# Two decode layers on one core: the last w2 chunk in 15 transfers, q in 12 slices, x added by five products

## The chip, the core and the metric

The kernel runs on one core of a Trainium2 chip. The time is that of the device, in microseconds, for one launch; three launches of the kernel before took 528.68, 529.14 and 530.48 us, so the median is 529.14. A core has TensorE (PE, matrix products), VectorE (DVE), ScalarE (ACT), GpSimd (POOL) and SyncE (SP, which here issues the loads), and 16 transfer engines that carry out what is issued. The inputs lie in HBM, the working memory (SBUF) and the accumulators of products (PSUM) have 128 partitions.

## The reference

Two layers, each an attention step and a feed-forward step on one token of width 640, with the same weights and the same cache in both layers. `setup_inputs` makes bf16 arrays; the key and value caches have 32 heads of 32768 rows by 192, of which the last 4096 are used.

```python
def _A_ref(x, k_cache, v_cache, wq, wo):
    B, Sq, D = x.shape                       # 1, 1, 640
    Hq, Dh = 32, 192
    Hkv, Sk = k_cache.shape[1], k_cache.shape[2]   # 32, 32768
    W = min(4096, max(256, Sk // 4))         # 4096
    q = (x @ wq).reshape(B, Sq, Hq, Dh).transpose(0, 2, 1, 3)
    k = k_cache[:, :, Sk - W:, :]
    v = v_cache[:, :, Sk - W:, :]
    scores = jnp.einsum("bhqd,bhkd->bhqk", q, k) * (Dh ** -0.5)
    p = softmax(scores, axis=-1)
    o = jnp.einsum("bhqk,bhkd->bhqd", p, v)
    return o.transpose(0, 2, 1, 3).reshape(B, Sq, Hq * Dh) @ wo

def _B_ref(x, w1, w3, w2):                   # 640x1536, 640x1536, 1536x640
    return (silu(x @ w1) * (x @ w3)) @ w2

x = A_x
x = x + _A_ref(layernorm(x), k_cache, v_cache, wq, wo)
x = x + _B_ref(layernorm(x), w1, w3, w2)
x = x + _A_ref(layernorm(x), k_cache, v_cache, wq, wo)
x = x + _B_ref(layernorm(x), w1, w3, w2)
```

## The kernel before

**Pages and loads.** Everything large goes through `arena`, an SBUF tile of 16 slots of 128 x 6144 bf16 (1.5 MB). One slot holds one page: a fifth of `wq`, the 4096 keys or values of one head, up to nine of the 48 chunks (128 x 640) of `wo`, or a piece of `w1`, `w3` and `w2`. The list `loads` has all pages of both layers in the order of use (lines 158 to 191). `refill` (193) takes the next page whenever a slot is free and issues its transfers on SP's queue at line 203; `done(key)` (218) frees a slot after the last product on its page and calls `refill`. Fourteen heads' keys stay in their slots for layer 1 (`RETAIN`), and one more is kept in PSUM (`stash`).

**The order of SP's queue.** `pin` keeps the order of the program on each engine, so SP issues in the order of `loads`. The tile framework gives the transfers eight completion semaphores in turn. An issue therefore waits for three things: its slot, a semaphore (until the load eight places before it has landed), and whatever wrote that slot before.

**The stages of a layer.** `layernorm` gives `xs`; `qproj` (247) multiplies it with the five `wq` pages: per page 16 products of 384 columns in `q_ps`, four abreast in the four column groups of TensorE (`tile_position`), then a copy (260), 12 small products that turn q (264 to 267) and a copy to `qt_sb` (268), from which `build_w` (270) puts the weights of the scores in `wst`. Per head, the keys are turned on VectorE (293) and multiplied; every four heads a softmax follows; the values follow six heads behind. `wo_proj` (392) multiplies the 48 chunks of `wo`. The head blocks are taken in the order `ORDER`, (3, 2, 1, 0) in layer 0 and (1, 0, 2, 3) in layer 1. The last three chunks (45 to 47) are not loaded in layer 1: they are multiplied with `wo5`, which layer 0 loaded for its own chunks 45 to 47, those of block 0.

**Openings.** `y_open` (383) opens the two accumulators of `wo_proj` and of layer 0's `w2` by eight products with `zero`, since later products write one row of each column group.

**The end.** In layer 1 `ffn` (412) prepares `ident`, a 128 x 128 f32 unit matrix in a free slot, on GpSimd; multiplies `w1` and `w3`; computes `htd`, the gated vector, and calls `last_rows` (466). That opens `f_ps` with four zero products, adds x by 20 small f32 products with `ident`, and multiplies `htd` with the twelve `w2` chunks in the order 0 to 3, 9 to 11 (in `keep` since layer 0), 4 to 8. Chunks 4 and 5, 6 and 7, and 8 are layer 1's last three loads (188). A copy (482) and one store of 4 rows of 160 (484) end the program.

Of the kernel before, what the change touches and what calls it, by code (L numbers as in the profile page):

```python
# [7 lines left out]
BF16 = mybir.dt.bfloat16  # L8
F32 = mybir.dt.float32
U32 = mybir.dt.uint32  # L10
ALU = mybir.AluOpType
# [4 lines left out]
P = 128  # L16
D = 640
NCH = 5
H = 32
# [4 lines left out]
HB = 4  # L24
NB = H // HB
PGW = 6144
# [15 lines left out]
def _ap(t, p0, npart, off, dims):  # L42
    ps = t.ap[0][0]
    return bass.AP(t.tensor, t.offset + p0 * ps + off, [[ps, npart]] + [list(d) for d in dims])
# [3 lines left out]
def kernel(  # L48
# [13 lines left out]
    nc = tc.nc  # L62
# [9 lines left out]
    m_ps = pss[:, MB:MB + MN]  # L72


    def pin(ins):
        tc.keep_in_program_order(ins)
        return ins

    def mm(*a, **k):
        return pin(nc.tensor.matmul(*a, **k))  # L80
# [17 lines left out]
    nc.gpsimd.memset(sel4[:], 0.0)  # L98
    nc.gpsimd.affine_select(out=sel4[:], in_=sel4[:], compare_op=ALU.not_equal, fill=1.0, base=0,
                            pattern=[[-32, 4]], channel_multiplier=1)  # L100
    sel16 = cst.tile([P, 4, 4], BF16, name="sel16")
    nc.gpsimd.memset(sel16[:], 0.0)
    nc.gpsimd.affine_select(out=sel16[:], in_=sel16[:], compare_op=ALU.not_equal, fill=1.0, base=0,
                            pattern=[[-32, 4], [-1, 4]], channel_multiplier=1)


    sel = cst.tile([P, 2, HB, 16], BF16, name="sel")
# [23 lines left out]
    zero = cst.tile([P, 32], BF16, name="zero")  # L131
    nc.gpsimd.memset(zero[:], 0.0)
    w20 = cst.tile([P, 768], BF16, name="w20")
    qt_sb = cst.tile([P, 2, 6, 16], BF16, name="qt_sb")
    rl = cst.tile([P, 1], F32, name="rl")


# [7 lines left out]
    loads = []  # L145
# [9 lines left out]
    def head(layer, g):  # L155
        return HG * ORDER[layer][g // HG] + g % HG

    for layer in range(2):
        for c in range(NCH):
            loads.append((("q", layer, c), [(0, PGW, wq_v[c])]))  # L160
        for i in range(H + LEAD):
            for kind, g, cache in (("v", i - LEAD, A_v_cache), ("k", i, A_k_cache)):
                if not 0 <= g < H:
                    continue
                h = head(layer, g)
                if kind == "k" and layer == 1 and h in RETAIN:
                    if h == STASH:
                        loads.append((("k", 1, h), []))
                    continue
                loads.append(((kind, layer, h),  # L170
                              [(0, PGW, cache[0, h, S0:SK, :].rearrange("(p t) d -> p (t d)", p=P))]))
        for w in range(6):
            parts, ci, end = [], 9 * w, min(9 * w + 9, 48)
            while ci < end:
                to = min(end, ci - ci % 12 + 12)
                parts.append((640 * (ci - 9 * w), 640 * (to - ci),
                              wo_v[ORDER[layer][ci // 12]][:, 640 * (ci % 12):640 * (ci % 12 + to - ci)]))
                ci = to
            if w < 5:
                loads.append((("o", layer, w), parts))  # L180
            elif layer == 0:
                assert len(parts) == 1 and parts[0][1] == 1920
                loads.append((None, [(wo5[:], parts[0][2])]))
        loads.append((("fa", layer), [(0, PGW, w1_v[:, 0:PGW])]))
        loads.append((("fb", layer), [(0, PGW, w3_v[:, 0:PGW])]))
        loads.append((("fc", layer), [(0, 1536, w1_v[:, PGW:]), (1536, 1536, w3_v[:, PGW:]),
                                      (3072, 2560, w2_v[:, 0:2560])]))
        fd = [(0, 3200)] if layer == 0 else [(0, 1280), (1280, 1280), (2560, 640)]
        loads.append((("fd", layer), [(o, n, w2_v[:, 2560 + o:2560 + o + n]) for o, n in fd]))
        if layer == 0:  # L190
            loads.append((None, [(keep[:], w2_v[:, 5760:7680])]))

    def refill():
        while loads and (free or loads[0][0] is None):
            key, parts = loads.pop(0)
            if key is None:
                for dst, src in parts:
                    pin(nc.sync.dma_start(out=dst, in_=src))
                continue
            s = free.pop(0)  # L200
            home[key] = s
            for off, n, src in parts:
                pin(nc.sync.dma_start(out=arena[:, s * PGW + off:s * PGW + off + n], in_=src))  # L203
            if not parts:
                stash(arena[:, s * PGW:s * PGW + PGW], False)

# [40 lines left out]
    def qproj(layer):  # L247
        q_ps = ps_a.tile([P, 512], F32, tag="a", name="q_ps")
        for c in range(NCH):
            pg = page(("q", layer, c))  # L250
            for c2 in range(4):
                for j in range(4):
                    hp = 4 * j + c2
                    mm(q_ps[32 * j:32 * j + 32, 0:384], lhsT=xs[:, c, 3 - c2:35 - c2],
                       rhs=pg[:, 384 * hp:384 * hp + 384],
                       start=(c == 0 and c2 == 0), stop=(c == NCH - 1 and c2 == 3),
                       tile_position=(0, 32 * j))
            done(("q", layer, c))
        q_sb = w20
        pin(nc.scalar.copy(out=q_sb[:, 0:384], in_=q_ps[:, 0:384]))  # L260
        qt_ps = m_ps[0:32].rearrange("p (h i c) -> p h i c", h=2, i=6)
        for hh in range(2):
            for it in range(6):
                be, par = divmod(it, 2)
                o = 64 * (3 * hh + be) + par
                mm(qt_ps[:, hh, it, :], lhsT=q_sb[:, o:o + 63:2],
                   rhs=sel16[:].rearrange("p j c -> p (j c)"), start=True, stop=True)
        pin(nc.vector.tensor_copy(out=qt_sb[0:32], in_=qt_ps[:]))  # L268

    def build_w(b, first):  # L270
        engs = (nc.gpsimd, nc.scalar) + ((nc.vector, nc.vector) if first else (nc.gpsimd, nc.scalar))
        for a in range(4):
            dst = _ap(wst[:], 32 * a, 32, 8 * a + HB - 1, [[382, HB // 2], [191, 2], [32, 6]])
            src = _ap(qt_sb[:], 0 if first else 32 * a, 32, HB // 2 * b, [[1, HB // 2], [96, 2], [16, 6]])
            pin((engs[a].copy if engs[a] is nc.scalar else engs[a].tensor_copy)(out=dst, in_=src))  # L275
        if first:
            for a in range(1, 4):
                pin(nc.vector.tensor_copy(out=qt_sb[32 * a:32 * a + 32], in_=qt_sb[0:32]))
# [104 lines left out]
    def y_open(name):  # L383

        y_ps = [ps_a.tile([P, 512], F32, tag="a", name=f"{name}{i}") for i in range(2)]
        for nh in range(2):
            for j in range(4):
                mm(y_ps[nh][32 * j:32 * j + 32, 0:320], lhsT=zero[:], rhs=ptm[:, 0:320],
                   start=True, stop=False, tile_position=(0, 32 * j))
        return y_ps  # L390

    def wo_proj(layer):
        y_ps = y_open("y_ps")
        for w in range(6):
            pg = page(("o", layer, w)) if w < 5 else wo5
            for cc in range(min(9, 48 - 9 * w)):
                ci = 9 * w + cc
                j = ci % 4
                for nh in range(2):
                    mm(y_ps[nh][32 * j:32 * j + 1, 0:320], lhsT=otd[:, ci:ci + 1],  # L400
                       rhs=pg[:, 640 * cc + 320 * nh:640 * cc + 320 * nh + 320],
                       start=False, stop=(ci >= 44), tile_position=(0, 32 * j))
            if w < 5:
                done(("o", layer, w))
        y_to_residual(y_ps)
# [6 lines left out]
    def ffn(layer):  # L412
        if layer == 1:
            assert not loads
            spare = free[0] * PGW
            ident = arena[:, spare:spare + 256].bitcast(F32)
            nc.gpsimd.memset(ident, 0.0)
            nc.gpsimd.affine_select(out=ident, in_=ident, compare_op=ALU.not_equal, fill=1.0, base=0,
                                    pattern=[[-1, P]], channel_multiplier=1)
        g_ps = ps_a.tile([P, 512], F32, tag="a", name="g_ps")  # L420
        u_ps = ps_a.tile([P, 512], F32, tag="a", name="u_ps")
        for ps, kind, c0, c1, off in ((g_ps, "fa", 0, 4, 0), (u_ps, "fb", 0, 4, 0),
# [42 lines left out]

    def last_rows(ident):
        f_ps = ps_a.tile([P, 512], F32, tag="a", name="f_ps")
        for j in range(4):
            mm(f_ps[32 * j:32 * j + 32, 0:160], lhsT=zero[:], rhs=ptm[:, 0:160], start=True, stop=False,
               tile_position=(0, 32 * j))  # L470
        for c in range(NCH):
            for j in range(4):
                mm(f_ps[32 * j:32 * j + 1, c:160:NCH], lhsT=xsq[:, c:c + 1], rhs=ident[:, 32 * j:32 * j + 32],
                   start=False, stop=False, tile_position=(0, 32 * j))
        for fcx in (0, 1, 2, 3, 9, 10, 11, 4, 5, 6, 7, 8):
            pg, off = w2_chunk(1, fcx)
            for j in range(4):
# [77 lines left out]
```

## Time and profile before

| what | value |
|---|---|
| three launches, us | 528.68, 529.14, 530.48 |
| profiled launch: span, us | 527.83 |
| mean granted clock of TensorE | 0.72 |
| busy: PE, DVE, ACT, POOL, us | 275.8, 256.5, 62.3, 14.3 |
| bytes read, MB | 221.6 |
| GB/s, mean over the span | 421 |
| GB/s, typical slice in the middle | 430 |
| last landing of `w2`, us | 524.36 |
| store issued, us | 525.08 |
| store landed, us | 526.74 |

The span is that of one profiled launch, from the program's first instruction to its last; the launches that were timed take 1.31 us more in the median. All times inside the launch count from the span's start. The landing times are those of the semaphores' updates; a load of 128 rows makes 16, one of each transfer engine, and has landed with the last. A line such as `L80 PE MATMUL` names line 80 of the kernel, the helper `mm` through which all products go, so products are told apart by the tiles they write. Of SP, the duration is that of issuing, not of the transfer.

### The profile page before, as it was taken

The page shows a single profiled execution, that of the slowest core. Times are in us where ns is not written, and L with a number is a line of the kernel's source. Part 1 is how long each engine was busy: PE and PEld are TensorE (multiplying, and loading weights), DVE is VectorE, ACT ScalarE, POOL GpSimd, SP SyncE. Part 2 cuts the span into 40 slices and gives each one's busy share as a digit, 9 for nine tenths or more (in the row PEclk, how much of TensorE's full clock was granted, in tenths as well). Part 3 has the DMA queues.
Part 4 walks back from the last instruction along what each step waited for, and adds up shares of the span by engine and source line. Part 5 has one row for each costly group of instructions (what it writes and reads, how often), then busy time and mean ns, then how long its engine had stood idle before and what let it go on. Part 6 is the DMA issues. An engine that isn't in the chain of part 4 may idle for free.

```text
span 527.8 us, 6132 instructions
## 1 busy us (share of the span) xinstructions
PE 275.8 (52%) x2487; PEld 113.9 (22%) x2487; DVE 256.5 (49%) x393; ACT 62.3 (12%) x192; POOL 14.3 (3%) x66
## 2 busy tenths in 40 slices
PE   2354644463645555455445446678254655446545
PEld 1111212121212221122112212233121322112212
DVE  1199676656656475754001139431475654753001
ACT  1002020111102020102000002022111120202000
POOL 4000000000000000000000000000000000000000
PEclk9997968676766776586556557888677886586556
DMA  8999999999999999999999999999999999999995
GB/s 350 430 429 429 428 431 429 427 431 429 427 431 431 430 425 432 430 426 425 416 433 422 430 430 401 431 431 427 430 429 427 429 430 431 430 428 428 424 432 215
DMA packets 22356, 221.97 MB, mean 421 GB/s; under 512 B 2617, under 2 KB 2745, under 8 KB 5177
## 3 DMA queue, kind: packets, MB, share of 16 engines
q1 hardware_dynamic: 22184, 221.59, 99.1%
q8 instruction: 19, 0.31, 0.2%
q14 instruction: 9, 0.07, 0.0%
q10 hardware_dynamic: 144, 0.00, 0.0%
HBM read 221.58 MB, written 0.00 MB: 420 GB/s over the span
## 4 chain that ended last, share of the span: by engine, by line
DMA 86%; PE 6%; DVE 5%; ACT 1%; issue 1%; SPq 0%; DVEq 0%; ACTq 0%
DMA arena<-in_A_k_cache_dram 54%; DMA arena<-in_A_v_cache_dram 14%; DMA arena<-in_A_wo_dram 8%; DMA arena<-in_A_wq_dram 6%; DMA arena<-in_B_w_dram 5%; DVE arena L293 4%; PE s_ps L80 3%; PE o_ps L80 2%; PE y_ps L80 1%; SPq L203 0%; ACT w L330 0%; PE pss L80 0%; PE q_ps L80 0%; DVE t L315 0%; PE g_ps L80 0%
## 5 line engine op out<-in xcount | busy, mean ns | idle before, releaser
L80 PE MATMUL s_ps<-arena,wst 128*32 128x512 bf16 x768 | 155.2, 518 | 172.7 <-DVE arena L293 86.4
L293 DVE STREAM_TRANSPOSE arena<-arena 128x1536 uint32<-128x1536 uint32 x100 | 171.2, 1754 | 77.3 <-DMA arena<-in_A_k_cache_dram 77.0
L80 PE MATMUL o_ps<-arena,ptm 128*8 128x384 bf16 (+1 forms) x1024 | 116.7, 425 | 11.4 <-DMA arena<-in_A_v_cache_dram 11.3
L80 PEld LDWEIGHTS <-wst 128*32 128x32 bf16 x768 | 52.9, 115 | 257.9 <-issue 226.7
L80 PEld LDWEIGHTS <-ptm 128*8 128x8 bf16 (+1 forms) x1024 | 41.0, 100 | 49.0 <-issue 38.8
L325 ACT ACTIVATE tb<-m 32x16 f32<-32x16 f32 x16 | 3.4, 215 | 280.6 <-DVE m L322 280.6
L343 ACT COPY ptm<-w 32x64 bf16<-32x64 bf16 x80 | 23.6, 295 | 44.5 <-PE o_ps L80 41.4
L80 PE MATMUL y_ps<-arena,otd 128*1 128x320 bf16 x180 | 16.5, 448 | 15.0 <-DMA arena<-in_A_wo_dram 15.0
L80 PE MATMUL q_ps<-arena,xs 128*32 128x384 bf16 x160 | 14.5, 519 | 17.5 <-DMA arena<-in_A_wq_dram 14.9
L376 DVE SCALAR_TENSOR_TENSOR w<-pss,rl,mask 64x192 bf16<-64x192 f32 x16 | 6.7, 416 | 31.7 <-PE pss L80 31.7
L275 POOL COPY wst<-qt_sb 32x24 bf16<-32x24 bf16 x30 | 8.4, 281 | 434.4 <-PE s_ps L80 315.8
L333 DVE STREAM_TRANSPOSE w<-w 64x512 bf16<-64x512 bf16 x16 | 11.3, 705 | 14.4 <-ACT w L330 14.4
L241 DVE CAST w<-y_ps 128x320 bf16<-128x320 f32 x3 | 1.5, 492 | 33.8 <-PE y_ps L80 33.8
L315 DVE TENSOR_REDUCE t<-s_ps 64x1 f32<-64x512 f32 x16 | 10.6, 663 | 12.2 <-PE s_ps L80 12.1
L80 PEld LDWEIGHTS <-xs 128*32 128x32 bf16 x240 | 8.8, 125 | 35.1 <-issue 23.0
L268 DVE CAST qt_sb<-pss 32x192 bf16<-32x192 f32 x2 | 0.7, 345 | 30.9 <-PE pss L80 30.9
L343 DVE COPY ptm<-w 32x64 bf16<-32x64 bf16 x48 | 10.0, 208 | 11.7 <-PE o_ps L80 10.4
L348 DVE RECIPROCAL rl<-pss 64x1 f32<-64x1 f32 x16 | 2.6, 165 | 20.5 <-PE pss L80 20.4
L80 PEld LDWEIGHTS <-otd 128*1 128x1 bf16 x192 | 6.4, 102 | 25.2 <-issue 21.1
L330 ACT ACTIVATE w<-s_ps,nbt 64x512 bf16<-64x512 f32 x16 | 10.9, 682 | 5.6 <-DVE nbt L327 5.6
L369 ACT CAST w<-o_ps 128x384 bf16<-128x384 f32 x16 | 7.7, 478 | 31.7 <-PE o_ps L80 23.3
L80 PE MATMUL pss<-w,sel 128*64 128x192 bf16 x32 | 6.0, 273 | 9.5 <-ACT w L369 6.4
(81 smaller groups left out, 107.8 us busy)
## 6 DMA issues: line engine op xcount, KB each, us to landing
arena<-in_A_v_cache_dram SPq DMA_DIRECT2D x64, 1536.0 KB, 29.2
arena<-in_A_k_cache_dram SPq DMA_DIRECT2D x50, 1536.0 KB, 29.2
arena<-in_A_wq_dram SPq DMA_DIRECT2D x10, 1536.0 KB, 9.5
arena<-in_A_wo_dram SPq DMA_DIRECT2D x6, 1440.0 KB, 20.8
arena<-in_B_w_dram SPq DMA_DIRECT2D x4, 1536.0 KB, 10.9
arena<-in_A_wo_dram SPq DMA_DIRECT2D x4, 960.0 KB, 16.5
arena<-in_A_wo_dram SPq DMA_DIRECT2D x4, 480.0 KB, 15.0
arena<-in_B_w_dram SPq DMA_DIRECT2D x4, 384.0 KB, 14.8
```

The source lines that it names most:

```text
L80: return pin(nc.tensor.matmul(*a, **k))
L241: pin(nc.vector.tensor_copy(out=y_sb[:, 320:640], in_=y_ps[1][:, 0:320]))
L275: pin((engs[a].copy if engs[a] is nc.scalar else engs[a].tensor_copy)(out=dst, in_=src))
L293: pin(nc.vector.transpose(x[:, w * sp:w * (sp + 1)].bitcast(U32), x[:, w * sp:w * (sp + 1)].bitcast(U32)))
L315: pin(nc.vector.reduce_max(out=t0[:, 0:1], in_=s_ps[0:64, :], axis=AX.X))
L325: pin(nc.scalar.mul(out=tb[32:64, :].rearrange("p (a z) -> p a z", a=4)[:, :, 0:HB], in_=mb, mul=-SCALE))
L330: pin(nc.scalar.activation(out=e[:], in_=s_ps[0:64, :], func=ACTF.Exp, bias=nbt[:, 0:1], scale=SCALE, accum_out=l[:]))
L333: pin(nc.vector.transpose(et[:], e[:]))
L343: pin((eng.copy if eng is nc.scalar else eng.tensor_copy)(out=dst, in_=src))
L348: pin(nc.vector.reciprocal(out=rl[half], in_=rl_ps[half]))
L369: pin(nc.scalar.copy(out=o_sb[:, 0:384], in_=o_ps[:, 0:384]))
L376: pin(nc.vector.scalar_tensor_tensor(out=om, in0=ot_ps[half], scalar=rl[half], in1=mask[half].unsqueeze(2).broadcast_to([64, 16, 12]), op0 ...
```

## The change

The diff has five parts.

- **Chunk 8 of `w2`.** The last load of layer 1 (128 rows of 640 columns, 160 KB) becomes 15 transfers of 9, 15, 14, 13, ... 2 rows of the same columns. `refill` takes parts with a first row and a number of rows.
- **q.** `qproj` takes q in 12 slices of 512 columns instead of 16 of 384: 12 products a page instead of 16, a copy of 512 columns, and 16 small turning products instead of 12. `sel16` becomes `sel12`, `qt_sb` has the layout head, part; `build_w` reads it so.
- **Openings.** `y_open` uses two products of 128 weight columns instead of eight of 32.
- **x at the end.** `last_rows` has no zero products; x comes by five f32 products of 128 weight columns with `xw` (x spread over columns, made on GpSimd by a memset and four copies) and a 128 x 32 `ident` (made by four selects), the first of which opens `f_ps`.
- **wo.** `wo_order` puts chunks 9 to 11 of block 3 last in layer 0, so that `wo5` holds those in both layers; layer 1's order is as it was.

```diff
+    def wo_order(layer):
+        last = ORDER[1][3]
+        kept = [12 * ORDER[layer].index(last) + e for e in (9, 10, 11)]
+        return [ci for ci in range(48) if ci not in kept] + kept
...
-        fd = [(0, 3200)] if layer == 0 else [(0, 1280), (1280, 1280), (2560, 640)]
-        loads.append((("fd", layer), [(o, n, w2_v[:, 2560 + o:2560 + o + n]) for o, n in fd]))
+        fd = [(0, 3200)] if layer == 0 else [(0, 1280), (1280, 1280)]
+        parts = [(o, n, w2_v[:, 2560 + o:2560 + o + n]) for o, n in fd]
+        if layer == 1:
+            p0 = 0
+            for rows in (9, 15, 14, 13, 12, 11, 10, 9, 8, 7, 6, 5, 4, 3, 2):
+                parts.append((2560, 640, w2_v[p0:p0 + rows, 5120:5760], p0, rows))
+                p0 += rows
+            assert p0 == P
+        loads.append((("fd", layer), parts))
...
-            for off, n, src in parts:
-                pin(nc.sync.dma_start(out=arena[:, s * PGW + off:s * PGW + off + n], in_=src))
+            for off, n, src, *rows in parts:
+                p0, np_ = rows or (0, P)
+                pin(nc.sync.dma_start(out=arena[p0:p0 + np_, s * PGW + off:s * PGW + off + n], in_=src))
...
-            for c2 in range(4):
+            for c2 in range(3):
                 for j in range(4):
-                    hp = 4 * j + c2
-                    mm(q_ps[32 * j:32 * j + 32, 0:384], lhsT=xs[:, c, 3 - c2:35 - c2],
-                       rhs=pg[:, 384 * hp:384 * hp + 384],
-                       start=(c == 0 and c2 == 0), stop=(c == NCH - 1 and c2 == 3),
+                    sl = 3 * j + c2
+                    mm(q_ps[32 * j:32 * j + 32, 0:512], lhsT=xs[:, c, 3 - c2:35 - c2],
+                       rhs=pg[:, 512 * sl:512 * sl + 512],
+                       start=(c == 0 and c2 == 0), stop=(c == NCH - 1 and c2 == 2),
                        tile_position=(0, 32 * j))
...
-            for j in range(4):
-                mm(y_ps[nh][32 * j:32 * j + 32, 0:320], lhsT=zero[:], rhs=ptm[:, 0:320],
-                   start=True, stop=False, tile_position=(0, 32 * j))
+            mm(y_ps[nh][:, 0:320], lhsT=zero[:, 0:1].broadcast_to([P, P]), rhs=ptm[:, 0:320], start=True, stop=False)
...
-            ident = arena[:, spare:spare + 256].bitcast(F32)
+            ident = arena[:, spare:spare + 64].bitcast(F32)
             nc.gpsimd.memset(ident, 0.0)
-            nc.gpsimd.affine_select(out=ident, in_=ident, compare_op=ALU.not_equal, fill=1.0, base=0,
-                                    pattern=[[-1, P]], channel_multiplier=1)
+            for j in range(4):
+                nc.gpsimd.affine_select(out=ident, in_=ident, compare_op=ALU.not_equal, fill=1.0, base=-32 * j,
+                                        pattern=[[-1, 32]], channel_multiplier=1)
+            xw = arena[:, spare + 64:spare + 64 + 1280].bitcast(F32)
+            nc.gpsimd.memset(xw, 0.0)
+            for j in range(4):
+                nc.gpsimd.tensor_copy(out=xw[32 * j:32 * j + 32, 32 * j:640:128], in_=xsq[32 * j:32 * j + 32, 0:NCH])
+            ident = (ident, xw)
...
-        for j in range(4):
-            mm(f_ps[32 * j:32 * j + 32, 0:160], lhsT=zero[:], rhs=ptm[:, 0:160], start=True, stop=False,
-               tile_position=(0, 32 * j))
+        eye, xw = ident
         for c in range(NCH):
-            for j in range(4):
-                mm(f_ps[32 * j:32 * j + 1, c:160:NCH], lhsT=xsq[:, c:c + 1], rhs=ident[:, 32 * j:32 * j + 32],
-                   start=False, stop=False, tile_position=(0, 32 * j))
+            mm(f_ps[:, c:160:NCH], lhsT=xw[:, 128 * c:128 * c + 128], rhs=eye, start=(c == 0), stop=False)
```

More of the change, by code (lines that the diff above doesn't have):

```diff
@@ L100 @@
                             pattern=[[-32, 4]], channel_multiplier=1)
[L101 to L104, printed above, removed]
+    sel12 = cst.tile([P, 4, 3], BF16, name="sel12")
+    nc.gpsimd.memset(sel12[:], 0.0)
+    nc.gpsimd.affine_select(out=sel12[:], in_=sel12[:], compare_op=ALU.not_equal, fill=1.0, base=0,
+                            pattern=[[-32, 4], [-1, 3]], channel_multiplier=1)
     sel = cst.tile([P, 2, HB, 16], BF16, name="sel")
@@ L133 @@
     w20 = cst.tile([P, 768], BF16, name="w20")
-    qt_sb = cst.tile([P, 2, 6, 16], BF16, name="qt_sb")
+    qt_sb = cst.tile([P, H, 6], BF16, name="qt_sb")
     rl = cst.tile([P, 1], F32, name="rl")
@@ L172 @@
         for w in range(6):
[L173 to L178, printed above, removed]
+            parts = []
+            for at, ci in enumerate(wo_order(layer)[9 * w:9 * w + 9]):
+                blk, e = ORDER[layer][ci // 12], ci % 12
+                if parts and parts[-1][2] == blk and parts[-1][3] + parts[-1][1] == e:
+                    parts[-1][1] += 1
+                else:
+                    parts.append([at, 1, blk, e])
+            parts = [(640 * at, 640 * n, wo_v[blk][:, 640 * e:640 * (e + n)]) for at, n, blk, e in parts]
             if w < 5:
@@ L259, in qproj @@
         q_sb = w20
[L260 to L268, printed above, removed]
+        pin(nc.scalar.copy(out=q_sb[:, 0:512], in_=q_ps[:, 0:512]))
+        qt_ps = m_ps[0:32].rearrange("p (s n) -> p s n", s=12)
+        for blk in range(8):
+            for par in range(2):
+                o = 64 * blk + par
+                mm(qt_ps[:, :, 2 * blk + par], lhsT=q_sb[:, o:o + 63:2],
+                   rhs=sel12[:].rearrange("p j c -> p (j c)"), start=True, stop=True)
+        pin(nc.vector.tensor_copy(out=qt_sb[0:32].rearrange("p h i -> p (h i)"),
+                                  in_=qt_ps.rearrange("p s n -> p (s n)")))
     def build_w(b, first):
@@ L272, in build_w @@
         for a in range(4):
-            dst = _ap(wst[:], 32 * a, 32, 8 * a + HB - 1, [[382, HB // 2], [191, 2], [32, 6]])
-            src = _ap(qt_sb[:], 0 if first else 32 * a, 32, HB // 2 * b, [[1, HB // 2], [96, 2], [16, 6]])
+            dst = _ap(wst[:], 32 * a, 32, 8 * a + HB - 1, [[191, HB], [32, 6]])
+            src = _ap(qt_sb[:], 0 if first else 32 * a, 32, 6 * HB * b, [[6, HB], [1, 6]])
             pin((engs[a].copy if engs[a] is nc.scalar else engs[a].tensor_copy)(out=dst, in_=src))
@@ L395, in wo_proj @@
             pg = page(("o", layer, w)) if w < 5 else wo5
-            for cc in range(min(9, 48 - 9 * w)):
-                ci = 9 * w + cc
-                j = ci % 4
+            for cc, ci in enumerate(wo_order(layer)[9 * w:9 * w + 9]):
+                n = 9 * w + cc
+                j = n % 4
                 for nh in range(2):
@@ L401, in wo_proj @@
                        rhs=pg[:, 640 * cc + 320 * nh:640 * cc + 320 * nh + 320],
-                       start=False, stop=(ci >= 44), tile_position=(0, 32 * j))
+                       start=False, stop=(n >= 44), tile_position=(0, 32 * j))
             if w < 5:
```

## The prediction

> **What bounds the kernel now.** I read the page's table of the span in slices first, then the chain of waits over its last 28 us, then the sync queue's two issuing lines, then the stages at the end, and last the timeline of the final row.
>
> ```profile
> span 527.8 us, 6132 instructions
> ...
> DMA  8999999999999999999999999999999999999995
> ...
> q1 hardware_dynamic: 22184, 221.59, 99.1%
> ```
>
> The transfer engines are busy from the second slice to the last but one; the one sync (SP) queue carries all 221.59 MB. Faster arithmetic in the middle buys nothing: only the bytes, the first 2 us and what follows the last bytes count.
>
> ```profile
> 486.47 21.06 DMA arena<-in_A_wo_dram
> 507.53 0.02 issue
> 507.54 0.02 SPq L203
> 507.56 0.03 issue
> 507.59 16.45 DMA arena<-in_B_w_dram
> 524.04 0.04 issue
> 524.08 0.31 PE f_ps L80 x8
> ```
>
> The chain's end is transfer to transfer: a `wo` load lands at 507.53, SP wakes, and only then issues the second last `w2` load (chunks 6 and 7), which lands at 524.04. The loads take eight completion semaphores in turn, and each issue first waits until the load eight places before it has landed. The load of chunk 8, the last, is the next link: it waits for the eighth before it (landed 510.94), is issued at 511.01 and lands at 524.36. Its issue is 13 us early, so that wait costs nothing now.
>
> ```profile
> L203 SPq DMA_DIRECT2D arena<-in_B_w_dram x14: 327/328/328, 268.4 to 511.0; - x14
> L484 SPq DMA_DIRECT2D out_dram<-w x1: 657/657/657, 525.1 to 525.1; - x1
> ```
>
> An issue holds SP for 328 ns (least, median, greatest duration of the group). The only issue of few rows, the output's four, holds it 657 ns. From its start at 525.08 to its landing at 526.74 are 1.66 us, and that is the trace's only small transfer with nothing ahead of it.
>
> ```profile
> 519.00:520.00 1.00, 1.00 (x16) 0.43 (x9) 0.00 (x0) 0.00 (x0) 0.00 (x0) 0.50 1.01 410
> 520.00:521.00 1.00, 0.95 (x11) 0.27 (x6) 0.22 (x1) 0.48 (x1) 0.00 (x0) 0.50 0.80 315
> 521.00:522.00 1.00, 0.62 (x36) 0.59 (x39) 0.45 (x2) 0.18 (x1) 0.00 (x0) 0.54 0.53 205
> 522.00:523.00 1.00, 0.39 (x40) 0.26 (x31) 0.72 (x5) 0.00 (x0) 0.00 (x0) 1.00 0.28 97
> 523.00:524.00 1.00, 0.67 (x36) 0.52 (x29) 0.00 (x0) 0.00 (x0) 0.00 (x0) 1.00 0.08 19
> ```
>
> Each row is one microsecond; the last three columns are granted clock, DMA share and GB/s. The 16 transfer engines do not finish together: the share falls from 1.01 to 0.08 over 4 us. The semaphore records of the chunk-8 load say it per engine: 16 landings from 520.55 to 524.36, mean 521.99. The latest engine carried a 16 KB instruction fetch of 0.92 us at 522.01 in the packet records; without it the latest would be the next one, 523.71, and for the load of chunks 6 and 7 it would be 523.30 instead of 524.04.
>
> ```profile
> 514.33 0.50 PEld L80 LDWEIGHTS pss<-xsq,onesD 128*128 128x128 f32 x2 [0.54 <-DVE xsq L223]
> ...
> 521.57 0.33 PE L80 MATMUL f_ps<-ptm,zero 128*32 128x160 bf16 x4
> ...
> 521.68 0.60 PE L80 MATMUL f_ps<-arena,xsq 128*1 128x32 f32 x40
> ...
> 522.88 0.64 PEld L80 LDWEIGHTS <-htd 128*1 128x1 bf16 x37 [0.74 <-DVE htd L449]
> 524.70 0.32 DVE L482 CAST w<-f_ps 128x160 bf16<-128x160 f32 x1 [1.87 <-PE f_ps L80]
> ```
>
> The opening of `f_ps` (zero products, then x) ends at 522.28 and TensorE waits until 522.88 for `htd`: 0.6 us of slack.
>
> **The change, part by part.**
>
> *Chunk 8 as 15 transfers.* Bytes and rows are the same (128 rows of 1280 B, 55 ns each in the packet records), but SP issues 15 loads for one, each waiting for the load eight before it. The first keeps its place (issue 511.0). The 15-row one waits for the `w1` page (514.56), the next for `w3` (518.23), then for the four pieces after it: 519.22, 520.15, 521.67, 522.46. Those seven are queued while the transfer engines still run, so they cost nothing. The eighth (9 rows) waits for the load of chunks 6 and 7, and that lands on its slowest engine: I take 523.30, with 524.04 as the other bound. Behind it in SP's queue stand the seven remaining loads (8, 7, ... 2 rows) and the output store; TensorE's chunk-8 products wait for all fifteen. The waits of those seven loads are for the small loads queued earlier, over by then.
>
> So from 523.30 SP issues eight loads in a row. Pitch of an issue: below, 0.37 (328 ns and the gap to the next start, as at 7.09 and 7.47 us, two loads without a wait between); above, 0.70 (657 ns of the four-row store, and the 0.04 gap). Below both, an issue that cost in proportion to its rows would be 0.06 (328 ns x 44/128 rows over eight, and the gap), which the four-row row speaks against. The seven loads at the program's start, issued back to back, start from 0.74 to 3.83: 0.52 each. The two nearest rows, one in count of rows, one in being loads in a burst, are 0.70 and 0.52; I take 0.61 between them. Last issue starts at 523.30 + 0.03 + 7 x 0.61 = 527.60; landing 1.66 later: 529.26, against 524.36. **+4.9 us.** Ends: pitch 0.37 gives 527.58 (+3.2); pitch 0.70 and 524.04 give 530.63 (+6.3).
>
> *x by five products.* Each is f32 with 128 weight columns; the layernorm's has the same weight shape, two loads in 0.50 at granted clock 0.50. Ten loads: 2.5 us, or 1.25 if the clock goes to 1.00 as it does at 522.0. From 521.57 the opening would end between 522.8 and 524.1 instead of 522.28, and beyond 522.88 it delays the 36 products of chunks 0 to 5 and the keep chunks (0.79 us now) and those of 6 and 7 (0.24). TensorE would then reach chunk 8 between 523.9 and 525.1. Cover: the chunk-8 wait until 529.26. Without it, it is a rival below. Its preparation on GpSimd (a memset five times the 0.21 us one, four small selects of about 0.2, four copies like the 0.28 ones) starts with the residual at 513.92 at the latest for the copies and ends by about 515.5, 6 us before its use; GpSimd has nothing queued behind it.
>
> *q in 512 columns.* Per page 12 products instead of 16, the same columns streamed (four abreast, 3 x 512 for 4 x 384), 1.47 us now; then 16 small products for 12 (0.49 us now, +0.16), and a copy of 512 columns for 384 (0.48, +0.12). In both layers this runs while the loads stream at a DMA share of 1.01; if that cover were gone the price is 0.3 us a layer. The openings of `y_ps` (8 products to 2, 0.72 us) are followed by `wo` waits of 1 to 3 us, so their saving is nothing. The reorder of `wo` in layer 0 moves the same bytes in as many loads: nothing. TensorE's program is about 100 instructions shorter by the end, so the fetch of 522.01 probably falls out, which is why 523.30 stands above.
>
> **Sum.** 529.26 plus the time from landing to the end, as now 527.83 - 524.36 = 3.47, gives a span of 532.73: +4.9. The median of the runs is 529.14, 1.31 above the span; adding 4.9 gives **534.0 us**, its own range 532.4 (+3.2) to 535.4 (+6.3).
>
> **Rivals.**
>
> *The issues are cheap, and the opening decides.* With the proportional pitch (0.06) the last rows land near 525.4 and TensorE arrives between 523.9 and 525.1; the last products end about 0.8 later than now (524.67): 529.9. For it: 128-row issues have constant 328 ns, so the price of fewer rows is not shown. Against: the 657 ns.
>
> *The staircase balances the engines, and the waits do not bite.* Suppose n rows go one to each of n transfer engines, always counted from the same one. Then the first two engines get 15 rows, the next 14, and the last none. If the engines at the far end are the late ones, the latest loses 8 rows (8 x 52 ns = 0.41) and the fetch. The gain is capped by TensorE: `htd` at 522.88 plus 0.79 + 0.24 reaches chunk 8 at 523.9 to 524.1, against 524.40 for the last four products now: at most 0.5. It decides if the eighth issue starts before about 518.0 (523.9 less 7 x 0.61 and 1.66), so if it need not wait for the load of chunks 6 and 7. Time: 528.6, not slower. For it: the 4 us spread. Against: the eight-semaphore wait is in the chain itself, and the lateness looks like fetches that wander, not like an order of engines. The Trainium skill ("DMA: Bandwidth & Descriptors", the section on why a DMA increments its semaphore by 16) has this spreading as a rule: n rows run on n engines, the lowest-numbered. The store's semaphore agrees, with four late updates from 526.68 to 526.74; which engine is late, no run here shows. By that rule alone the result would be the 528.6 of this rival.
>
> **How the numbers follow.** The wait and eight issues: 0.82. Cheap issues, opening decides: 0.08. Balance: 0.05. The rest, 0.05, is gains or losses that I do not see. A measurement here tells 0.3% (1.6 us) from no change. The first case is slower throughout; the next two are within 0.3%. So slower 0.82, same 0.13, faster 0.05. Range: 530.4, near the second case, to 536.0, the first one's upper end and the 0.6 by which medians may shift.
>
> **What would show it.** Right: seven of the fifteen issues by 522.8, then eight in a burst from about 523.3, at a pitch of 0.4 to 0.7; the last landing at 527.6 to 530.6; the chain of waits ending in `w2` loads and SP's issuing line; TensorE idle before the last four products. Wrong: a burst before 522, chunk-8 products that follow the others without a wait, or `f_ps` loads of x ending after the last landing.

## The result, and the profile after

Four launches of the changed kernel took 531.72 to 532.62 us, median **532.01**; four of the kernel before 528.68 to 530.48, median 529.13. The ratio is 1.0053 (95% interval 1.0038 to 1.0069), so the change costs 2.9 us, with 2.0 to 3.7 as the interval. The direction and the range held; the forecast of 534.0 was 2 us too high. The 532.01 also lies below 532.4 to 535.4, the range that the sum gave by itself.

From the page of the changed kernel, the span, the busy share of the transfer engines in 40 slices, and the sync queue:

```profile
span 529.9 us, 5995 instructions
...
DMA  8999999999999999999999999999999999999993
...
q1 hardware_dynamic: 22296, 221.59, 98.7%
```

The bytes are the same and the engines are as busy as before, up to the last slice: there the digit is 3 where it was 5. What was added lies behind the bytes. The chain of waits over the last 23 us (start, duration, what) shows where:

```profile
506.94 15.82 DMA arena<-in_B_w_dram
522.77 0.02 issue
522.78 0.27 SPq L218
523.05 0.04 issue
523.10 0.29 SPq L218
...
524.79 0.27 SPq L218
525.06 0.04 issue
525.11 1.27 DMA arena<-in_B_w_dram
526.37 0.04 issue
526.41 0.33 PE f_ps L80 x4
```

The load of chunks 6 and 7 lands at 522.77, and only then does SP issue the eighth small load; eight issues follow one another to 525.11, the last (2 rows) lands 1.27 later, and TensorE's last four products start at once. The two groups of issues of SP (least, median and greatest ns):

```profile
L218 SPq DMA_DIRECT2D arena<-in_B_w_dram x28: 251/327/354, 269.0 to 525.1; - x28
L499 SPq DMA_DIRECT2D out_dram<-w x1: 619/619/619, 527.2 to 527.2; - x1
```

The 251 to 354 of the loads are those of the small ones; 128 rows have 327 or 328 as before. So a load of few rows holds SP about as long as one of many, and the 619 ns belong to the store. In the table by microsecond (PE busy, PEld, DVE, ACT, POOL, then clock, DMA share, GB/s) the price is empty time:

```profile
522.00:523.00 1.00, 0.90 (x31) 0.79 (x34) 0.28 (x2) 0.00 (x0) 0.00 (x0) 0.79 0.19 54
523.00:524.00 1.00, 0.84 (x28) 0.49 (x16) 0.00 (x0) 0.00 (x0) 0.00 (x0) 0.50 0.13 29
524.00:525.00 1.00, 0.00 (x0) 0.00 (x0) 0.00 (x0) 0.00 (x0) 0.00 (x0) 0.50 0.10 27
525.00:526.00 1.00, 0.00 (x0) 0.00 (x0) 0.00 (x0) 0.00 (x0) 0.00 (x0) 0.50 0.06 18
```

From 524 on no engine computes, and 16 transfer engines move 27 and 18 GB/s where the middle of the run has 430. The timeline of the same stretch (start, duration, engine, line, operation; in brackets the idle time before it and what ended it):

```profile
520.99 1.27 PE L80 MATMUL f_ps<-arena 128*128 128x32 f32 x10
...
522.12 0.19 DVE L468 TENSOR_TENSOR htd<-gut,ex 128x12 bf16<-128x12 f32 x1
522.37 1.13 PEld L80 LDWEIGHTS <-htd 128*1 128x1 bf16 x44 [0.21 <-DVE htd L468]
...
526.41 0.30 PE L80 MATMUL f_ps<-arena,htd 128*1 128x160 bf16 x4 [2.58 <-DMA arena<-in_B_w_dram]
```

x by five products (ten passes of 128 weight columns) takes 1.27 us and ends 0.05 before TensorE could have `htd`: hidden. The last line has the wait of 2.58 us for the last small loads.

Span against span the change costs 529.89 - 527.83 = 2.06, median against median 2.88. The time of a launch is 1.65 to 2.1 above its span in the launches after the prediction that have both: 1.82 in the changed kernel's, 1.9 in the median of the kernel before. By 1.9 the profiled launch of before took about 529.73, 0.6 above its kernel's median, and that of the changed kernel, 531.72, lies 0.3 below its own. 2.06 + 0.6 + 0.3, less the 0.1 between 1.9 and 1.82, is the 2.88 but for rounding.

### The profile page after: what moved, and what is told of

Read it like the earlier page. It is cut to its first block, busy times and chain, and to the rows that moved or that the text cites. A ratio compares the mean times of both kernels' runs of the same rounds, so it can differ in the third digit from the quotient of the medians.

```text
span 529.9 us, 5995 instructions
## 1 busy us (share of the span) xinstructions
PE 281.3 (53%) x2403; PEld 114.0 (22%) x2403; DVE 256.4 (48%) x393; ACT 62.5 (12%) x192; POOL 16.1 (3%) x74
## 4 chain that ended last, share of the span: by engine, by line
DMA 82%; PE 8%; DVE 7%; ACT 1%; SPq 1%; issue 1%; DVEq 0%; ACTq 0%
DMA arena<-in_A_k_cache_dram 51%; DMA arena<-in_A_v_cache_dram 15%; DMA arena<-in_A_wo_dram 7%; DMA arena<-in_B_w_dram 5%; PE s_ps L80 5%; DVE arena L308 5%; DMA arena<-in_A_wq_dram 3%; PE o_ps L80 2%; SPq L218 1%; PE y_ps L80 1%; ACT w L345 1%; PE q_ps L80 1%; DVE t L330 0%; ACT wst L290 0%; PE pss L80 0%
## 5 line engine op out<-in xcount | busy, mean ns | idle before, releaser
L80 PE MATMUL s_ps<-arena,wst 128*32 128x512 bf16 x768 | 157.3, 526 | 163.1 <-DVE arena L308 80.5
L80 PE MATMUL o_ps<-arena,ptm 128*8 128x384 bf16 (+1 forms) x1024 | 115.0, 429 | 16.4 <-DMA arena<-in_A_v_cache_dram 16.3
L80 PE MATMUL q_ps<-arena,xs 128*32 128x512 bf16 x120 | 14.7, 623 | 19.0 <-DMA arena<-in_A_wq_dram 16.4
L80 PE MATMUL y_ps<-arena,otd 128*1 128x320 bf16 x180 | 17.0, 458 | 14.7 <-DMA arena<-in_A_wo_dram 14.7
L80 PEld LDWEIGHTS <-xs 128*32 128x32 bf16 x200 | 7.0, 119 | 38.1 <-issue 28.5
```

## The experiments

All medians below stand against launches of the kernel before on the same chip in the same batch (23, 27 and 33 launches; medians 529.02, 529.13 and 528.90). All kernels but that of the last row are the changed kernel with another list of rows for chunk 8, so that they hold the other four parts of the change. Two further runs, which also halve a `w3` page, stand at the end of the experiments.

| rows of the transfers of chunk 8 | median, us | against before | 95% of the ratio |
|---|---|---|---|
| 128 | 529.21 | +0.19 | 0.9987 to 1.0014 |
| 128, second time | 528.98 | +0.08 | 0.9989 to 1.0007 |
| 63, 63, 2 | 528.86 | -0.04 | 0.9989 to 1.0006 |
| 48, 16 x5 | 529.84 | +0.71 | 1.0002 to 1.0019 |
| 63, 27, 18, 9, 9, 2 | 529.74 | +0.84 | 1.0002 to 1.0020 |
| 32, 16 x6 | 530.09 | +1.07 | 1.0010 to 1.0030 |
| 32, 16 x5, 14, 2 | 530.03 | +0.90 | 1.0011 to 1.0029 |
| 16 x8 | 530.97 | +1.95 | 1.0023 to 1.0049 |
| 16 x7, 4 x4 | 531.07 | +1.94 | 1.0024 to 1.0049 |
| 9, 15, 14 ... 2, alone on the kernel before | 532.65 | +3.63 | 1.0053 to 1.0078 |

### Which part of the change costs

The changed kernel with one load for chunk 8:

```diff
-            for rows in (9, 15, 14, 13, 12, 11, 10, 9, 8, 7, 6, 5, 4, 3, 2):
+            for rows in (128,):
```

> The changed kernel with chunk 8 as one transfer of 128 rows; all other edits stay. Theory (eight issues in a row behind the landing of chunks 6 and 7): the last landing falls to about 523.2, TensorE ends the other 44 products at about 523.8 and then decides, so 2.6 us below the changed kernel: 529.4. Rival A (small transfers cost by their number, wherever they are issued): 529.1, the time before. Rival B (the loss comes from the other edits: q, openings, x): no change, about 532.0.

The kernel before with the 15 transfers alone (q, openings, x and `wo` as they were):

```diff
-        fd = [(0, 3200)] if layer == 0 else [(0, 1280), (1280, 1280), (2560, 640)]
+        fd = [(0, 3200)] if layer == 0 else [(0, 1280), (1280, 1280)]
...
+            for rows in (9, 15, 14, 13, 12, 11, 10, 9, 8, 7, 6, 5, 4, 3, 2):
+                parts.append((2560, 640, w2_v[p0:p0 + rows, 5120:5760], p0, rows))
```

> The kernel before with chunk 8 in the 15 transfers and no other edit. Theory: the last landing is that of chunks 6 and 7 (523.3 to 524.0 in the profile of before) plus 0.03, seven issues of 0.33 and 1.27, so 527.0 to 527.6 instead of 524.4, and the time 2.7 to 3.3 above before: 531.8 to 532.4. Rival A: 532.0 too. Rival B: 529.1, no change.

One load: 529.21 (+0.19, the interval holds 1), 0.2 below the theory's 529.4 and 0.1 above the 529.1 of rival A (cost by number). The split alone: 532.65 (+3.63), 0.25 above the upper end of the theory's 531.8 to 532.4. Rival B, by which the other edits cost, falls in both. The four other parts together are worth nothing that can be measured, and the split is worth all of it; its chain is that of the changed kernel, with the load of chunks 6 and 7 at 522.89, eight issues and the last landing at 526.49. The +3.63 and the +2.88 have overlapping intervals, so no gain of the other parts is read from their difference.

### Where the price begins: seven and eight transfers

If the wait for chunks 6 and 7 were all, seven transfers would be free, and an eighth would cost one landing.

```diff
-            for rows in (9, 15, 14, 13, 12, 11, 10, 9, 8, 7, 6, 5, 4, 3, 2):
+            for rows in (32, 16, 16, 16, 16, 16, 16):
```

> The changed kernel with chunk 8 in seven transfers of 32 and 6 x 16 rows: none of them is eighth behind the load of chunks 6 and 7, so all are issued before it lands. Theory: no loss against one transfer, 529.4 (the same as with one transfer within 0.3). Rival A: 6/14 of 2.9 us above one transfer, so 1.2 above it.

```diff
-            for rows in (9, 15, 14, 13, 12, 11, 10, 9, 8, 7, 6, 5, 4, 3, 2):
+            for rows in (16, 16, 16, 16, 16, 16, 16, 16):
```

> The changed kernel with chunk 8 in eight transfers of 16 rows: exactly one, the eighth, waits for the landing of chunks 6 and 7. Theory: one issue and 1.27 us behind that landing, so the last landing at about 524.1, just past TensorE's 523.8: 0.3 above seven transfers, 529.7, with the last products waiting for the eighth transfer. Rival A: 0.2 above seven, both 1.2 to 1.4 above one transfer.

Both miss. Seven cost 0.9 more than one, and eight 1.3 more than forecast. The seventh was issued at 522.56, behind the load of chunks 4 and 5, and landed at 524.39. Of the eighth, this is the chain of waits:

```profile
506.91 15.92 DMA arena<-in_B_w_dram
522.83 0.02 issue
522.84 2.48 DMA arena<-in_B_w_dram
525.32 0.04 issue
```

The landing took 2.48 us where the 2-row load took 1.27. Fifteen of its sixteen updates came between 524.17 and 524.48, and one at 525.32. The packet records have an instruction fetch on one transfer engine at 523.30, for 0.95 us. A packet of the eighth load starts at 524.23, as the fetch ends; its fifteen others had started by 524.13. So two costs seemed to be missing: one that comes with the number of transfers, and one from the fetch.

### The fetch, and the price of a late issue

Eight transfers again, but the last one of two rows, which leaves out most engines:

```diff
-            for rows in (9, 15, 14, 13, 12, 11, 10, 9, 8, 7, 6, 5, 4, 3, 2):
+            for rows in (32, 16, 16, 16, 16, 16, 14, 2):
```

> The changed kernel with chunk 8 in eight transfers, the eighth of 2 rows (32, 5 x 16, 14, 2) instead of 16. With 16 rows, 15 engines landed at 524.2 to 524.5 and one at 525.3, and a 16 KB instruction fetch of 0.95 us began at 523.3. Theory with the fetch (the late engine is the one that fetches TensorE's last instructions, and two rows on two engines mostly miss it): last landing at 524.1, 0.9 to 1.2 below the eight of 16: 529.8 to 530.1. Theory without it (the wait and the issue alone): the same as eight of 16, 531.0.

Eleven transfers, the last four of four rows:

```diff
-            for rows in (9, 15, 14, 13, 12, 11, 10, 9, 8, 7, 6, 5, 4, 3, 2):
+            for rows in (16, 16, 16, 16, 16, 16, 16, 4, 4, 4, 4):
```

> The changed kernel with chunk 8 in eleven transfers (7 x 16 and 4 x 4 rows): four issues behind the landing of chunks 6 and 7 instead of eight. Theory: last landing 522.8 + 0.03 + 3 x 0.31 + 1.27 = 525.0, 1.4 below the changed kernel's 526.4: 530.6. Rival A (by number of transfers, 10/14 of 2.9): 531.2.

Eight with a small last one: 530.03, 1.05 less over before than eight of 16 rows. The forecast with the fetch (529.8 to 530.1) holds, the one without it (531.0) falls. In its chain the 2-row load lands 1.26 after its issue, as in the changed kernel:

```profile
523.45 0.02 issue
523.47 1.26 DMA arena<-in_B_w_dram
524.73 0.04 issue
```

Eleven: 531.07, nearer to the 531.2 of rival A than to the theory's 530.6. The last landing came at 525.34 for the expected 525.0, and TensorE began its last products 0.31 after it, where 0.04 is the gap in the changed kernel; for that the trace gives no reason. For the theory speaks the step from eight to eleven: 1.04, where three further issues at the changed kernel's pitch of 0.33 are 1.0. The late issues start at 522.90, 523.24, 523.53 and 523.87, which is that pitch again; the last lands 1.47 later. And the count alone does not set the price: eight with a small last one cost no more than seven (+0.90 and +1.07). That gives the price of the burst: 0.33 for each issue after the first behind the load of chunks 6 and 7, then one landing of 1.3 to 1.5.

### What each transfer costs even when it is issued early

Six transfers: none waits for chunks 6 and 7, nor for the pair of chunks 4 and 5.

```diff
-            for rows in (9, 15, 14, 13, 12, 11, 10, 9, 8, 7, 6, 5, 4, 3, 2):
+            for rows in (48, 16, 16, 16, 16, 16):
```

> The changed kernel with chunk 8 in six transfers (48 and 5 x 16 rows). Seven cost 0.9 us against one transfer, and there the seventh was issued at 522.56, behind the landing of chunks 4 and 5, and landed 1.83 us later. Theory (a transfer is late where the landing eight places before it plus 1.3 us comes after the engines have run dry, about 523.2): the sixth waits for the load of chunks 0 to 3 (521.2 to 521.7), so 522.5 to 523.0, and nothing is lost: 529.2 to 529.5, as with one transfer. Rival A (each further transfer costs, wherever it is issued, 0.9 us for six): 530.0.

529.84, nearer to the rival's 530.0 (each transfer costs) than to the theory's 529.2 to 529.5. The sixth load is issued at 521.23 and lands at 523.86. The updates of the six loads' semaphores, the last three of each (us from the start of the span), say why:

```
load (rows)     third last   last two
1 (48)            522.05     522.98 523.01
2 (16)            522.24     523.16 523.18
3 (16)            522.44     523.33 523.35
4 (16)            522.64     523.50 523.52
5 (16)            522.84     523.67 523.69
6 (16)            523.04     523.84 523.86
```

Two transfer engines report 0.8 to 0.9 us behind the others in every load, and one load after another 0.17 us apart. The third last updates come 0.2 apart as well, so the spacing is not that of the late engines alone; it is on them that it ends last. Nor is it the spacing of the packets: the last small packets follow one another at 0.058, and the last packet record before the store's ends at 522.79, 1.07 ahead of the last update. So a transfer in the queue has a price of 0.17 to 0.2 of its own at each engine, whatever it carries: on the late ones six have 6 x 0.17 = 1.02, where the one transfer of 8 rows an engine takes 8 x 52 ns = 0.41. The difference, an estimate of 0.6, is near the measured 0.71. The launch that was profiled took 529.06, the least of its eleven, so its trace shows the spacing but not the loss itself.

### Can the rows be kept off the late engines?

In the changed kernel's trace the nested transfers (9, 15, 14 ... rows) give each engine's place in the order in which rows are dealt. The load of chunks 6 and 7 landed last on the 10th and the 11th of them (522.72, 522.77); the others had landed by 522.21. A theory of two fixed late engines follows: transfers that go to the first nine alone would avoid them. 63 rows are 9 x 7.

```diff
-            for rows in (9, 15, 14, 13, 12, 11, 10, 9, 8, 7, 6, 5, 4, 3, 2):
+            for rows in (63, 27, 18, 9, 9, 2):
```

> The changed kernel with chunk 8 in six transfers again, but of 63, 27, 18, 9, 9 and 2 rows, which nine transfer engines carry (all but the last, two). In the six of 48 and 16 rows the last updates of the semaphores came from two engines alone, 0.17 us from transfer to transfer, and in the changed kernel those two were the tenth and eleventh by count of rows. Theory (each further transfer costs 0.17 us on these two late engines, 0.06 on the others): without them no loss against one transfer, last landing of chunk 8 by 523.1; 529.1 to 529.3. Rival A (each transfer costs, on whatever engine): 529.8 as with the other six.

```diff
-            for rows in (9, 15, 14, 13, 12, 11, 10, 9, 8, 7, 6, 5, 4, 3, 2):
+            for rows in (63, 63, 2):
```

> The changed kernel with chunk 8 in three transfers of 63, 63 and 2 rows: the idea of the staircase (no rows of chunk 8 for the engines that are behind) without any wait behind the load of chunks 6 and 7. Theory: chunk 8 lands by 523.0, before the other products end (523.6 to 523.9), so TensorE's chain decides: 529.0 to 529.2, the same as with one transfer. Rival (the last landing still decides with one transfer): 0.3 to 0.5 less than with one transfer, 528.8.

A load of 63 rows made nine updates. The Trainium skill ("DMA: Bandwidth & Descriptors", "Why a DMA increments its semaphore by 16 and not by 1") has the rule: the number of engines is the largest up to 16 that divides the rows, and they are the lowest-numbered; the trace agrees in the number. But the six-transfer kernel took 529.74, as the rival had it (529.8) and not the theory (529.1 to 529.3). In its trace two late engines were among the first nine: the updates of the 63 rows end with 523.65 and 523.94, and the next three loads' last ones came at 524.15, 524.35 and 524.55, again 0.2 apart; the fifth ended at 524.75. The 0.06 that the theory allowed the other engines was the spacing of packets; their updates for the five loads are 0.17 to 0.2 apart too (522.92, 523.10, 523.28, 523.46, 523.63). With three transfers the late pair was among the last seven (its updates for chunks 6 and 7 at 523.23 and 523.30), the first nine had the first 63 rows by 522.25, and the time was still 528.86, like before. The rival's forecast of 528.8 fits that number too, but one transfer in the same batch took 528.98, and the difference is within the noise. The late engines were not the same ones in these traces. With one trace for each kernel it stays open whether they go with the kernel or with the launch; no fixed list of rows followed them.

Two transfers of 63 rows and one of 2 cost nothing; six cost 0.8. That, too, goes with the number of transfers.

### Is there a version that beats both?

With one load for chunk 8 the chain of the second run of it leaves the `w2` loads altogether:

```profile
497.06 21.10 DMA arena<-in_B_w_dram
518.16 0.04 issue
...
521.47 2.36 PE f_ps L80 x58
523.83 0.02 issue
```

> The changed kernel with chunk 8 as one transfer once more, to be compared on the same chip: 529.2, as before within 0.1%.

It hangs on the landing of layer 1's `w3` page at 518.16 and TensorE's work behind it, 5.7 us; the last `w2` load lands at 523.50, just ahead of the end of that work. So the page was halved, that TensorE might begin sooner, with chunk 8 as one load and as three:

```diff
-        loads.append((("fb", layer), [(0, PGW, w3_v[:, 0:PGW])]))
+        loads.append((("fb", layer), [(0, PGW, w3_v[:, 0:PGW])] if layer == 0 else
+                      [(0, PGW // 2, w3_v[:, 0:PGW // 2]), (PGW // 2, PGW // 2, w3_v[:, PGW // 2:PGW])]))
```

> A try to beat both: the changed kernel with chunk 8 as one transfer and layer 1's w3 page in two transfers of half its columns, so that TensorE has 8 products less (0.78 us) to do when the second half lands. Theory: with one transfer the end hung on TensorE's chain behind the w3 landing (519.0 to 524.8), no longer on the last landing; so up to 0.8 less until the last landing (523.2 and 0.4 for the last products) decides: 528.7, 0.5 below one transfer. Rival (the last landing decides anyway): 529.2, no change.

> Both ends eased: w3's page of layer 1 in two halves (TensorE reaches chunk 8 some 0.8 us earlier) and chunk 8 in 63, 63 and 2 rows (landing by 523.0). Each alone was or should be no change, since the other end then decides. Theory (two ends near each other): together 0.3 to 0.6 below before, 528.6. Rival (what varies is the stream of loads before, and neither end): 529.1, no change.

529.31 (+0.18, 0.9991 to 1.0009) and 528.89 (-0.01, 0.9991 to 1.0009): neither gains, and both forecasts of a gain (528.7 and 528.6) fall. In the second one's chain the last products wait for a `w2` load that lands at 523.70. With one load for chunk 8 the two ends, of TensorE's chain and of the last landing, lie within some tenths of each other, which fits that relief of one is met by the other; that this is the whole reason is argued, not shown. Nothing that ran is faster than the kernel before.

## Why the prediction was right in direction and too high

**The mechanism was right, but two of its signs failed.** The first seven issues came early (510.58, 514.19, 517.85, 518.77, 519.68, 521.21, 522.00), the other eight in a burst behind the landing of chunks 6 and 7, TensorE stood idle before its last four products, and the chain ends in `w2` loads and SP's issuing line. The split alone reproduces the loss, and the other four parts alone lose nothing. But the pitch was to be 0.4 to 0.7 and the last landing 527.6 to 530.6; they were 0.33 and 526.37. The time lies in the stated 530.4 to 536.0 because that reached below the sum's own range, down to the case of cheap issues; and 0.8 us of the miss was taken back by luck, as the last point of the list below tells.

**The sum was too high in three terms**, in the spans of the two profiled launches:

| term | predicted | measured | off by |
|---|---|---|---|
| chunks 6 and 7 land | 523.30 | 522.77 | -0.53 |
| first to last of eight issues | 7 x 0.61 = 4.27 | 7 x 0.33 = 2.32 | -1.95 |
| last issue to landing | 1.66 | 1.27 | -0.39 |
| landing to end of span | 3.47 | 3.52 | +0.05 |
| gap from landing to first issue | 0.03 | 0.01 | -0.02 |
| span | 532.73 | 529.89 | -2.84 |

- **The pitch** is the step that failed. I set it between the four-row store's 0.70 and the 0.52 of the opening burst, as the rows nearest in count of rows and in being a burst. The measured 0.33 lies below even the lower bound of 0.37, which was the row of a load without a wait. The store was the wrong neighbour: kind of transfer (a load into SBUF against a store to HBM) outweighed the number of rows. An issue in proportion to its rows (0.06) was wrong as well, so the rival of cheap issues never came to decide: between 2 and 9 rows an issue of the burst takes 251 to 295 ns.
- **The landing** had the same wrong neighbour: 1.66 is the store's, 1.26 to 1.27 that of a 2-row load with nothing ahead of it, in three kernels.
- **The landing of chunks 6 and 7** came 0.5 earlier than on the latest undisturbed engine before; it lies between 522.77 and 523.45 in the runs whose chain shows it and which have that wait.
- **What lies around the span**, 1.31, was a median set against the span of another launch. Within one launch it is 1.8 to 1.9; by that the profiled launch of before was 0.6 slower than its median, and the changed kernel's was 0.3 faster than its own. Together this took back 0.8 of the 2.84, so that the forecast missed by 2.0.

**The instruction fetch did not fall out** with the hundred instructions that the change saves: it moved from 522.01 to 523.49. No cost of it shows here: the updates of the nine-row load, issued just before it, came from 524.06 to 524.30, and the burst ends 2 us later. With an eighth load on all 16 engines it cost about 1 us. That the burst escapes it because its loads run on few engines is argued, not shown.

**x, q, openings, `wo`**: each as predicted, together +0.1 to +0.2 within the interval. The ten passes of x took the lower of the two values, 1.27, since the clock stood at 1.00 there; 120 products of 512 columns took 14.7 us for 14.5.

**The rival of balance** fell on both its conditions. The waits bite. And the lateness has no order that the staircase matches: the engine that gets none of the small transfers was among the earliest (520.14), and late engines stood in other places in the two kernels made to test it.

**What the prediction lacked** is the price of a transfer that is issued early. "Those seven are queued while the transfer engines still run, so they cost nothing" is wrong: six cost 0.7 to 0.8, seven 1.1. The 0.17 us that each takes on a late engine explains most of it by the estimate above, which no run tests by itself. In the changed kernel that is covered by the burst, for the queued loads report last at 523.74, and the burst lands at 526.37. The kernel of seven transfers, which has no burst, has it as its loss.

## What to carry to other kernels

Cutting the last load of a full queue into pieces moves no byte sooner: every piece behind the last big landing costs one issue (here 0.33 us), the last of them its whole time from issue to landing (1.27), and the pieces ahead of it cost some 0.17 each on the engines that end last; up to three were free. Price an unseen transfer by a row of the same kind, load by load and store by store, before one of the same size. And set the median of launches against the profiled launch's own time, not against its span.

## What the runs showed of the hardware that was not expected

- A load of 2 rows holds SP for 231 to 251 ns and one of 128 for 327 or 328; a store of 4 rows, 619 to 657.
- In the kernels with chunk 8 split, two or three of the sixteen transfer engines, in one kernel five, ended 0.5 to 1.1 us behind the others, and not the same ones in all. With one load for chunk 8 none stood out so, other than by the fetch, unless the `w3` page was halved. Engines with small transfers in their queue, late or not, report them some 0.15 to 0.2 us apart, though the last packets follow at 0.058, so that the reports fall up to 1 us behind the packets. Why they come so slowly stays open.
- The end has one instruction fetch of 16 KB, for 0.88 to 1.45 us on one transfer engine. In the kernels with the five products it starts 1.0 to 1.1 us after TensorE's first product with `htd`, in the two with the old opening 0.9 and 1.4 us ahead of it. It goes with the place in TensorE's program rather than with the loads; whose fetch it is, no run settles.
